# Attention and gated MoE on one core: batches of one row block of four head pairs, and x copied to SBUF

## The chip, the cores and the metric

One NeuronCore of one Trainium2 chip runs the whole program in one launch. The metric is device time in microseconds from the start to the end of one execution. The time before is the median of three runs, 314.85 us, and smaller is better. All data are fp32; the order of the instructions on each engine is fixed when the program is built.

## The reference

Two parts follow one another. The first is causal-local attention with 8 heads over 4 sequences of 768 rows; the second gates a projection of its output by a short causal convolution. Cut to what matters:

```python
# q, k, v: (B=4, H=8, S=768, D=64), n_global = 8, n_local = 96
scores = q @ k.T / 8 ;  rel = row - col
keep = (col < n_global) | ((rel >= 0) & (rel < n_local))
scores += -slope[h] * dist            # dist: |rel|, n_local for global columns
a = softmax(where(keep, scores, -1e9))
x = concat_heads(a @ v)               # (4, 768, 512)
gate = sigmoid(sum_k conv_w[k] * x[t - 4 + k])    # 5 taps, per channel
out = (gate * (x @ w_val)) @ w_out    # (4, 768, 512)
```

## The kernel before

Of each block of 128 rows only a window of 232 columns of the scores is needed: 96 columns before the block, 8 global ones, and the block's own 128. The first block of a sequence needs its own 128 columns alone. One **step** is one row block of one head pair: 4 sequences x 6 blocks x 4 pairs = 96 steps. For each step the two heads' scores go into PSUM, VectorE (DVE) adds the bias and takes the row minimum (`add_bias`, L454; the scores are negated), ScalarE (ACT) takes the exponential with its row sum (`expo`, L464), GpSimd (POOL) or DVE guards the sum (L471), DVE inverts it (L474), POOL or DVE normalises (`norm`, L479), TensorE (PE) transposes (L489 to L495, one PSUM bank), and ACT or DVE copies the transposed p out as `a` (L155 on ACT, L157 on DVE).

A **group** is three steps: three row blocks (half a sequence) of one head pair. Scores (`scores`, L446) and attention times v (`pv`, L515 to L522) run as one batch per group, 32 batches each. From the fifth group on, the `pv` batch of group g - 2 is put directly ahead of the score batch of group g. The result x^T of a group, 128 channels by 384 rows, stands in a single PSUM bank (`x`), with 4 columns of history in front (`hist_in`). From that bank are made:

- `xh`, x rounded to the matmul's float32r (L155 or L157), and `xl`, what rounding left out (L608);
- the five taps of the convolution: the first on ACT or DVE (L618, L620), four on DVE that accumulate into `gate` (L616);
- the last 4 columns, copied to `hist` for the next half.

The bank is free for the next group's `pv` when all of these are done. A **phase** is half a sequence, four groups, 8 phases in all. When a phase's four pairs are there, `val` (L675) is 48 matmuls of 384 columns in three float32r products, ACT applies the sigmoid (L668), DVE multiplies `val` by the gate (L682), the product is split again (`gh`, `gl`, L688), and `out` (L695) is 36 matmuls of 512 columns; the result is copied to `ob` and stored. In the beginning the two weight matrices, given as float64, are converted in eight pieces on DVE, ACT, POOL and PE (L318 to L373).

The order is written by a planner, `Plan.order` (L85): every piece of work has an urgency, a list of what it waits for, and an assumed cost on each engine that may run it; the planner walks in time, gives each engine the most urgent piece that is ready, and chooses the engine that would end it first, with a handicap per engine (`SPARE`). The urgencies of the attention count in steps; those of the MoE part lag by `U_MOE`. The engines then run their lists strictly in that order. `plan.ring` makes a piece wait until a buffer's earlier user is done. All loads and stores go through SyncE's (SP) DMA queue. A run-time flag selects a slow general version for other window sizes, which isn't taken here.

Of the kernel before, what the change touches and what calls it, by code (L numbers as in the profile page):

```python
# [16 lines left out]
WARM = 8  # L17
S_B, PT_B, X_B = 4, 1, 1
U_D1, RAW_B = -6.0, 4
FILL_N, FILL_TO, U_F = 1, 1, -0.27  # L20
W_AT = (2.86, 3, 1.71, 9, 13.7, 16.76, 22, 22.5)
SPARE = {'vector': 0.6, 'gpsimd': -0.44, 'scalar': 0.0}
XH_B, GATE_B, P_B, T_B, A_B, V_B, W_B, WT_B = 7, 2, 5, 8, 9, 4, 2, 1
U_XE, U_XH, U_CV, CV_STEP = 0.7, -1.19, 0.01, 0.32
U_AM, U_EX, U_RC, U_PT, U_EV, U_MOE = 1.02, 1.72, 0.71, 1.89, 2.71, 18
LAG, ALONE = 2, 4
SLACK = 0.01
WO_PE, EARLY, XS_B, U_XO, U_CVE = 0, 0, 6, 0.5, 2.88
# [17 lines left out]
PER = P + NG  # L46
# [4 lines left out]

S_AT = {(k, j): (2 * j + k // 2, k % 2) for k in range(3) for j in range(2)}
# [80 lines left out]
def attention_moe(ctx, tc, qT, kT, kg, vw, v0, v, counts_in, wv, cw, wo, out):  # L133
# [8 lines left out]
    groups = [(b, hf, p) for b in range(B) for hf in range(2) for p in range(NP)]  # L142
    NGRP = len(groups)
    NSTEP = NGRP * HB
# [37 lines left out]
    hist = one.tile([P, NP, HIST], F32, name="hist")  # L182
# [13 lines left out]
    def base(kb):  # L196
        return 0 if kb == 0 else P + PER * (kb - 1)

    def kcols(hf):
        return (0, base(HB)) if hf == 0 else (base(HB) - TAIL, base(NB))  # L200

    def width(s):
        g, k = divmod(s, HB)
        return P if groups[g][1] == 0 and k == 0 else WIN

    def load(g, which):

        b, hf, p = groups[g]
        if which == "rk":
            src, (lo, hi), n = kT[b, p], kcols(hf), 512  # L210
        else:
            src, (lo, hi), n = qT[b, p], (hf * HT, (hf + 1) * HT), HT
        nc.sync.dma_start(tile_of((which, g), [P, n], F32, which, RAW_B)[:, : hi - lo], src[:, lo:hi])

    def load_v0(g):
        b, hf, p = groups[g]
        nc.sync.dma_start(tile_of(("v0", g), [P, 2, D], F32, "v0", 4), v0[b, p])

    def load_v(g):
        b, hf, p = groups[g]  # L220
        t = tile_of(("v", g), [P, HB, 2, 2, D], F32, "v", V_B)
        if hf == 0:
            nc.sync.dma_start(t[:, 1:], vw[b, p, :, : HB - 1])
        else:
            nc.sync.dma_start(t, vw[b, p, :, HB - 1 :])

    for g, (b, hf, p) in enumerate(groups):
        lo, hi = kcols(hf)
        for which, n in (("rk", hi - lo), ("rq", HT)):
            key = ("L" + which, g)  # L230
            plan.add(key, 3 * g + U_L, {SP: 0.5}, lambda e, g=g, which=which: load(g, which),
                     plan.ring(which, RAW_B, key, [("S", g)]), P * n * 4)
        if hf == 0:
            key = ("LV0", g)
            plan.add(key, 3 * g + U_LV, {SP: 0.5}, lambda e, g=g: load_v0(g),
                     plan.ring("v0", 4, key, [("PV", g)]), P * 2 * D * 4)
        key = ("LV", g)
        plan.add(key, 3 * g + U_LV + 0.1, {SP: 0.5}, lambda e, g=g: load_v(g),
                 plan.ring("v", V_B, key, [("PV", g)]), P * (HB - 1 + hf) * 4 * D * 4)
# [12 lines left out]
    for g in range(FILL_TO):  # L252
        for i in range(3):
            plan.add(("F", 3 * g + i), 3 * g + i + U_F, {PE: 0.22 * FILL_N}, lambda e: zeros(FILL_N),
                     [("S", g), ("WARM",)] + [("AM", 3 * g + i, 1)])
# [54 lines left out]
    for h in range(H):  # L310
        for part, cost in enumerate(({DVE: 0.13, POOL: 0.27}, {DVE: 0.19, POOL: 0.36})):
            plan.add(("BIAS", h, part), 3 * (h // 2) + part - 1 + 0.1 * (h % 2), cost,
                     lambda e, h=h, part=part: biases(e, h, part), [("DIST", part)])


    def f64_abs(raw, n, nm):
        y = tile_of((nm, "y"), [P, DM], F32, "wy", WT_B)[:, :n]
        nc.scalar.activation(y, raw[:, :, 1].bitcast(F32), AF.Abs)  # L318

    def f64_op(raw, n, nm, k):  # L320
# [9 lines left out]
        elif k == 2:  # L330
            h = tile_of((nm, "h"), [P, DM], I32, "wh", WT_B)[:, :n]
# [4 lines left out]
        else:  # L336
            r = tile_of((nm, "r"), [P, DM], F32R if by_pe(nm[1]) else F32, "wr", WT_B)[:, :n]
# [37 lines left out]
    def by_pe(i):  # L375
        return i < NC or WO_PE

# [5 lines left out]
    plan.ring("moe", 2, ("WARM",), [("WARM",)] + [("F", s) for s in range(3 * FILL_TO)])  # L383
    for i in range(2 * NC):
# [584 lines left out]
```

## Time and profile before

| | |
|---|---|
| median of three runs | 314.85 us (313.56 to 316.6) |
| the profiled execution | 314.51 us |
| its span on the engines | 312.7 us |
| granted TensorE clock, mean | 0.98 |
| PE busy (matmul) | 287.5 us, 92% |
| DVE busy | 230.8 us, 74% |
| ACT busy | 227.8 us, 73% |
| POOL busy | 148.1 us, 47% |
| DMA | 36.27 MB, mean 116 GB/s |

The profile is of one execution; its times are microseconds from the start of the span. Matmuls overlap in TensorE's pipeline, so their durations add up to more than the time that they take, and the distance between two starts is what one costs. A row of instructions gives start, duration, engine, line, operation, output and input, shape and count; a bracket at its end gives the engine's idle time before it and what ended it. A matmul in fp32 (scores, `pv`, transposes) is counted as two instructions, one in float32r as one.

### The profile page before, as it was taken

To read this page: it belongs to the slowest core of one execution; us is meant where nothing else is said; L and a number is where in the kernel's file an instruction comes from. 1 tells how busy PE (TensorE), PEld (TensorE's weight loads), DVE (VectorE), ACT (ScalarE), POOL (GpSimd) and SP (SyncE) were. 2 spreads that over 40 slices of the span, in tenths; PEclk is the share of its full clock that TensorE was granted. 3 is DMA by queue.
4 is the path that set the end of the run, shared out by engine and by line. 5 is a ranking of instruction groups with operands and counts; after the bars stand their busy time and mean duration, and the time that the engine had idled before them with its cause. 6 is when DMAs were issued, how large, how long until landed. Compare 5 with 4: busy or idle time off the path is not lost.

```text
span 312.7 us, 6857 instructions
## 1 busy us (share of the span) xinstructions
PE 287.5 (92%) x2140; PEld 230.5 (74%) x2140; DVE 230.8 (74%) x819; ACT 227.8 (73%) x634; POOL 148.1 (47%) x333
## 2 busy tenths in 40 slices
PE   8696958798999999999999999999999999999991
PEld 3463746676787777888788778888798778878981
DVE  4778897898678867879685768987698877796210
ACT  3677875996689778987797778877897779865320
POOL 5834556499444734384326442644434542550220
PEclk9999895999999999999999999999999999999998
DMA  6886553313444336313451355323444121001112
GB/s 190 272 275 212 185 170 106 115 51 88 159 128 118 106 101 201 114 47 85 132 189 53 114 155 170 85 85 102 152 146 111 50 85 69 2 2 48 55 39 73
DMA packets 21069, 36.27 MB, mean 116 GB/s; under 512 B 2592, under 2 KB 12832, under 8 KB 21024
## 3 DMA queue, kind: packets, MB, share of 16 engines
q1 hardware_dynamic: 21024, 35.75, 36.9%
q8 instruction: 19, 0.31, 0.4%
q14 instruction: 26, 0.21, 0.2%
HBM read 29.45 MB, written 6.29 MB: 114 GB/s over the span
## 4 chain that ended last, share of the span: by engine, by line
PE 51%; DVE 16%; ACT 14%; POOL 6%; issue 4%; POOLq 0%; ACTq 0%
PE o L695 14%; PE val L675 11%; DVE gate L616 7%; PE s L446 6%; PE x L519 5%; ACT p L464 5%; PE pt L492 4%; PE x L522 4%; POOL p L479 3%; DVE t L454 3%; PE pt L495 3%; DVE xl L608 2%; ACT gate L618 2%; ACT xh L155 1%; ACT gate L668 1%
## 5 line engine op out<-in xcount | busy, mean ns | idle before, releaser
L464 ACT ACTIVATE p<-t,mins 128x232 f32<-128x232 f32 (+1 forms) x192 | 90.4, 472 | 18.2 <-DVE mins L454 16.0
L479 POOL TENSOR_SCALAR p<-p,rs 128x232 f32<-128x232 f32 (+1 forms) x177 | 83.6, 484 | 35.1 <-DVE rs L474 24.7
L616 DVE SCALAR_TENSOR_TENSOR gate<-x,cwt,gate 128x384 f32<-128x384 f32 x128 | 78.2, 611 | 1.9 <-ACT xh L155 1.2
L454 DVE CUSTOM_DVE_ANT_0 t<-s,bias 128x232 f32<-128x232 f32 (+1 forms) x192 | 68.3, 371 | 0.5 <-PE s L446 0.5
L471 POOL TENSOR_SCALAR sm<-sm 128x2 f32<-128x2 f32 x93 | 18.9, 203 | 91.7 <-ACT p L464 87.3
L155 ACT COPY a<-pt 128x464 f32<-128x464 f32 (+1 forms) x87 | 44.6, 513 | 21.1 <-PE pt L495 18.5
L446 PE MATMUL s<-rk,rq 64*128 64x232 f32 (+1 forms) x384 | 47.5, 384 | 1.6 <-DMA rq<-in_qT 1.6
L675 PE MATMUL val<-xh,wvh 128*128 128x384 f32 x128 | 46.8, 366 | 1.4 <-DVE g L682 0.8
L492 PE MATMUL pt<-ident,p 104*128 104x104 f32 x160 | 33.2, 278 | 10.9 <-POOL p L479 9.4
L675 PE MATMUL val<-xh,wvl 128*128 128x384 f32 x128 | 43.2, 337 | 0.0
L675 PE MATMUL val<-xl,wvh 128*128 128x384 f32 x128 | 43.1, 337 | 0.0
L695 PE MATMUL o<-woh,gh 128*128 128x512 f32 x96 | 41.3, 430 | 1.0 <-DVE g L682 1.0
L492 PEld LDWEIGHTS pt<-ident,p 104*128 104x128 f32 x160 | 20.3, 144 | 29.2 <-POOL p L479 17.9
L446 PEld LDWEIGHTS s<-rk,rq 64*128 64x128 f32 x384 | 34.7, 203 | 8.2 <-DVE rs L474 1.9
L695 PE MATMUL o<-wol,gh 128*128 128x512 f32 x96 | 38.0, 396 | 1.4 <-POOL wol L361 1.4
L688 POOL TENSOR_TENSOR gl<-g,gh 128x384 fp32r<-128x384 f32 x30 | 30.5, 1018 | 18.1 <-ACT gh L155 17.2
L695 PE MATMUL o<-woh,gl 128*128 128x512 f32 x96 | 37.8, 394 | 0.0
L474 DVE RECIPROCAL rs<-sm 128x2 f32<-128x2 f32 x96 | 15.8, 164 | 28.2 <-POOL sm L471 27.0
L464 ACT ACTIVATION_READ_ACCUMULATOR p<-t,mins 128x1 f32 x192 | 36.4, 190 | 0.0
L519 PE MATMUL x<-a,v 128*64 128x128 f32 x320 | 33.2, 286 | 0.0
L495 PE MATMUL pt<-ident,p 128*128 128x128 f32 x160 | 31.9, 281 | 0.0
L522 PE MATMUL x<-a,v 104*64 104x104 f32 x320 | 29.0, 260 | 0.0
(164 smaller groups left out, 463.1 us busy)
## 6 DMA issues: line engine op xcount, KB each, us to landing
rq<-in_qT SPq DMA_DIRECT2D x32, 192.0 KB, 3.5
v<-in_vw SPq DMA_DIRECT2D x16, 384.0 KB, 3.2
out<-ob SPq DMA_DIRECT2D x24, 256.0 KB, 2.1
v<-in_vw SPq DMA_DIRECT2D x16, 256.0 KB, 2.8
rk<-in_kT SPq DMA_DIRECT2D x16, 252.0 KB, 3.5
rk<-in_kT SPq DMA_DIRECT2D x16, 200.0 KB, 3.2
w<-in_wv SPq DMA_DIRECT2D x4, 512.0 KB, 4.6
w<-in_wo SPq DMA_DIRECT2D x4, 512.0 KB, 3.7
```

The source lines that it names most:

```text
L155: nc.scalar.copy(dst, src)
L446: nc.tensor.matmul(T["s", g, k, j][:, :n], T["rq", g][r, k * P : (k + 1) * P], T["rk", g][r, c0 : c0 + n], start=True, stop=True)
L454: nc.vector.tensor_tensor_reduce(out=t[:, :n], in0=T["s", s // HB, s % HB, j][:, :n], in1=bias[:, h, :P] if n == P else bias[:, h, P:], op ...
L464: nc.scalar.activation(T["p", s][:, j, :n], T["t", s, j][:, :n], AF.Exp, bias=mins[:, s, j : j + 1], scale=-1.0, accum_out=T["sm", s][:, j ...
L479: engine(e).tensor_scalar(out=pr, in0=pr, scalar1=rs, scalar2=1.0, op0=ALU.mult, op1=ALU.mult)
L492: nc.tensor.transpose(pt[:, j * QA : (j + 1) * QA], pr[:QA, j, :P], ident[:QA, :QA])
L495: nc.tensor.transpose(pt[:, c : c + P], pr[:, j, CA:], ident)
L519: nc.tensor.matmul(head(j, P), T["v", g][:, k, j, 1], a[:, 2 * QA + j * P : 2 * QA + (j + 1) * P], start=True, stop=False)
L522: nc.tensor.matmul(head(j, QA), T["v", g][:CA, k, j, 0], a[:CA, j * QA : (j + 1) * QA], start=False, stop=True)
L616: nc.vector.scalar_tensor_tensor(out=gt, in0=src, scalar=w, in1=gt, op0=ALU.mult, op1=ALU.add)
L675: nc.tensor.matmul(T["val", ph, m], (wvh, wvh, wvl)[r][:, c, m * P : (m + 1) * P], (T["xh", g], T["xl", g], T["xh", g])[r], start=(c == 0 ...
L695: nc.tensor.matmul(T["o", ph, k], (T["gh", ph, c], T["gl", ph, c], T["gh", ph, c])[r][:, cols], (woh, woh, wol)[r][:, c], start=(c == 0 an ...
```

## The change

The groups become **batches** of one row block of all four head pairs: 24 batches of four steps, in the order of the row blocks. Loads of q, k, v come as one transfer per batch each, from arrays that the host lays out so (`qb`, `k0`, `kb`, `vb`, `v0`). A batch of scores fills all eight halves of the four PSUM banks (before: six). `pv` of a batch writes a bank of 128 channels x 4 pairs x 128 rows, and this bank is copied at once to SBUF (`x_out`, 24 copies of 128x512 on ACT or DVE). `xh`, `xl` and the taps are then made from the copy `xs`, which holds a whole phase of three batches with its 4 columns of history; all three may now go to POOL as well, except the four accumulating taps. The convolution of a phase begins when its three batches are copied, and `val` waits for `xh` and `xl` of all three. The matmuls of scores, `pv`, transposes, `val` and `out` keep their shapes and number. The buffers for the weight conversion are taken from `ob`'s ring, and the options `WO_PE` and `EARLY`, which were off, are dropped. All urgencies, handicaps and buffer counts of the planner have other values, with one due time per batch (`U_ATT`) and per phase (`U_CVP`) added.

The core of the diff:

```diff
-U_D1, RAW_B = -6.0, 4
-SPARE = {'vector': 0.6, 'gpsimd': -0.44, 'scalar': 0.0}
-XH_B, GATE_B, P_B, T_B, A_B, V_B, W_B, WT_B = 7, 2, 5, 8, 9, 4, 2, 1
-U_AM, U_EX, U_RC, U_PT, U_EV, U_MOE = 1.02, 1.72, 0.71, 1.89, 2.71, 18
+U_D1, RK_B, RQ_B = -11.96, 3, 3
+SPARE = {'vector': 0.4, 'gpsimd': -1.07, 'scalar': -1.28}
+XH_B, XS_B, GATE_B, P_B, T_B, A_B, V_B, W_B, GL_B, OB_B = 2, 2, 2, 5, 7, 8, 3, 2, 4, 3
+U_AM, U_EX, U_RC, U_PT, U_EV, U_MOE = 1.48, 6.43, -11.79, -13.48, -2.33, 28
...
-    groups = [(b, hf, p) for b in range(B) for hf in range(2) for p in range(NP)]
+    batches = [(b, blk) for b in range(B) for blk in range(NB)]
...
+    def load_k(n):
+        b, blk = batches[n]
+        t = tile_of(("rk", n), [P, NP, WIN], F32, "rk", RK_B)
+        if blk == 0:
+            nc.sync.dma_start(t[:, :, :P], k0[b])
         else:
+            nc.sync.dma_start(t, kb[b, blk - 1])
...
+    def scores(n):
+        banks = [tile_of(("s", n, i), [P, 2, P * 2], F32, "s", S_B, psum) for i in range(4)]
+        w = width(n)
+        for p, j in [(p, j) for p in range(NP) for j in range(2)]:
             r = slice(j * D, (j + 1) * D)
+            x = T["s", n, p, j] = banks[2 * j + p // 2][:, p % 2]
+            nc.tensor.matmul(x[:, :w], T["rq", n][r, p], T["rk", n][r, p, :w], start=True, stop=True)
...
+    def s_deps(n):
+        deps = [("Lrk", n), ("Lrq", n)]
+        return deps + ([("AM", s, j) for s in range(NP * (n - 1), NP * n) for j in range(2)] if n else [])
+
+    def pv_deps(n):
+        deps = [("EV", s) for s in range(NP * n, NP * n + NP)] + [("LV", n)]
+        return deps + plan.ring("x", X_B, ("PV", n), [("XE", n)])
...
-    def x_high(e, g):
-        copy(e, tile_of(("xh", g), [P, HT], F32R, "xh", XH_B), x_of(g)[:, HIST:])
+    def x_out(e, n):
+        ph, _, cols = block(n)
+        copy(e, T["xs", ph][:, :, cols], T["x", n])
+
+    def x_high(e, n):
+        ph, dst, cols = block(n)
+        if n % HB == 0:
+            tile_of(("xh", ph), [P, NP, HT], F32R, "xh", XH_B)
+        copy(e, T["xh", ph][:, :, dst], T["xs", ph][:, :, cols])
...
-        gt, src, w = T["gate", ph][:, p], x_of(g)[:, k : k + HT], cwt[:, p, k : k + 1]
+        gt, src, w = T["gate", ph][:, p], T["xs", ph][:, p, k : k + HT], cwt[:, p, k : k + 1]
...
+            plan.add(key, u + U_XE, {ACT: 0.5, DVE: 0.6}, lambda e, n=n: x_out(e, n), [("PV", n), ("HI", ph)])
+            for name, at, cost, fn in (("XH", U_XH, {ACT: 0.5, DVE: 0.36, POOL: 0.75}, x_high),
+                                       ("XL", U_XL, {DVE: 0.62, POOL: 1.35}, x_low)):
...
+        for p in range(NP):
+            for k in range(TAPS):
+                key = ("CV", ph, p, k)
+                deps = [("CV", ph, p, k - 1)] if k else [("CW",)] + [("XE", n) for n in own]
...
+                plan.add(key, NP * (own[-1] + LAG) + U_CV + U_CVP[ph] + CV_P * p + CV_STEP * k,
+                         {DVE: 0.55} if k else {DVE: 0.37, ACT: 0.4, POOL: 0.75},
...
-                deps = [("XH", ph * NP + c), ("XL", ph * NP + c), ("WP", c), ("WH", c)]
+                deps = [(x, n) for n in range(HB * ph, HB * ph + HB) for x in ("XH", "XL")] + [("WP", c), ("WH", c)]
```

More of the change, by code (lines that the diff above doesn't have):

```diff
@@ L215, in load_v0, with width @@
[L215 to L223, printed above, removed]
-        else:
[L225 to L239, printed above, removed]
+    def width(n):
+        return P if batches[n][1] == 0 else WIN
@@ L554, in attention_moe, with s_cost, pv_cost @@
-    for g, (b, hf, p) in enumerate(groups):
-        for k in range(HB):
-            s = 3 * g + k
-            n = width(s)
-            full = n == WIN
+    def s_cost(n):
+        return (SCORES if width(n) == WIN else 0.22) * NP
+    def pv_cost(n):
+        return (0.395 if width(n) == WIN else 0.22) * NP
+    def s_deps(n):
[4 more added lines that the diff above has]
+        return deps + plan.ring("x", X_B, ("PV", n), [("XE", n)])
@@ new lines, in attention_moe @@
+    for n in range(NBAT + LAG):
+        h = n - LAG
+        u = NP * n + U_S
+        if n < NBAT and n < ALONE:
+            plan.add(("S", n), u, {PE: s_cost(n) + 2 * SWITCH}, lambda e, n=n: scores(n), s_deps(n))
+        if 0 <= h and n < ALONE or n >= NBAT:
+            plan.add(("PV", h), u, {PE: pv_cost(h) + 2 * SWITCH}, lambda e, h=h: pv(h), pv_deps(h))
+        if ALONE <= n < NBAT:
+            plan.add(("PV", h), u, {PE: pv_cost(h) + SWITCH}, lambda e, h=h: pv(h), s_deps(n) + pv_deps(h))
+            plan.add(("S", n), u, {PE: s_cost(n) + 2 * SWITCH}, lambda e, n=n: scores(n), s_deps(n) + [("PV", h)])
+            plan.follow(("S", n), ("PV", h))
@@ L559, in attention_moe @@
+    for n in range(NBAT):
+        for s in range(NP * n, NP * n + NP):
+            p = s % NP
+            full = width(n) == WIN
+            due = s + U_ATT[n]
             for j in range(2):
                 key = ("AM", s, j)
[L561 to L562 removed]
+                plan.add(key, due + U_AM, {DVE: 0.32 if full else 0.21}, lambda e, s=s, j=j: add_bias(s, j),
+                         [("S", n), ("BIAS", 2 * p + j, int(full))] + plan.ring("t", T_B, key, [("EX", s, j)]))
@@ L604, in x_high, with hist_in @@
-    def x_high(e, g):
-        copy(e, tile_of(("xh", g), [P, HT], F32R, "xh", XH_B), x_of(g)[:, HIST:])
-    def x_low(e, g):
-        engine(e).tensor_sub(tile_of(("xl", g), [P, HT], F32R, "xl", XH_B), x_of(g)[:, HIST:], T["xh", g])
-    def conv(e, g, k):
-        ph, p = divmod(g, NP)
+            plan.add(key, due + U_EV, {ACT: 0.5 if full else 0.3, DVE: 0.58 if full else 0.33},
+                     lambda e, s=s: evac_pt(e, s), [("PT", s)] + plan.ring("a", A_B, key, [("PV", n)]))
+    def hist_in(e, ph):
+        x = tile_of(("xs", ph), [P, NP, HIST + HT], F32, "xs", XS_B)
+        if ph % 2 == 0:
+            nc.gpsimd.memset(x[:, :, :HIST], 0.0)
+        else:
+            copy(e, x[:, :, :HIST], T["xs", ph - 1][:, :, HT:])
```

303 lines of the change are left out of this document (117 added, 186 removed).

## The prediction

> **What bounds the kernel now.** I read the page's engine line first, then the span cut into stages, and then the instructions of TensorE one after the other. The columns of the stage rows are: stretch, its length, busy us of PE, weight loads, DVE, ACT and POOL, the granted clock, and the DMA share.
>
> ```profile
> span 312.7 us, 6857 instructions
> PE 287.5 (92%) x2140; PEld 230.5 (74%) x2140; DVE 230.8 (74%) x819; ACT 227.8 (73%) x634; POOL 148.1 (47%) x333
> ...
> 4.90:81.67 76.77, 63.13 (x420) 46.27 (x420) 64.35 (x215) 55.83 (x162) 49.60 (x95) 0.93 0.51 166
> 81.67:145.85 64.18, 62.80 (x516) 51.85 (x514) 50.56 (x191) 52.87 (x150) 31.21 (x77) 1.00 0.41 120
> 145.85:212.26 66.41, 65.53 (x527) 54.15 (x525) 51.01 (x190) 53.03 (x151) 30.01 (x75) 1.00 0.41 120
> ...
> 269.88:306.40 36.52, 36.08 (x224) 30.45 (x222) 18.09 (x50) 16.36 (x37) 9.96 (x16) 1.00 0.11 38
> ```
>
> I cut the stages where the score batch of group 0, 8, 16, 24 and 31 begins, so the first three hold eight groups each (the fourth, with seven, is left out; the last is the tail). From 81.67 us on PE is busy 98 to 99% of the time, eight groups cost 64.2 to 66.4 us, and the tail, nearly all MoE, is full too. **The middle and the tail are bound by PE.** The first stage is not: 76.8 us for eight groups, although it holds fewer PE instructions, 420 against 516 and 527. There DVE has the highest share, 64.35 of 76.77 us (84%), and the clock is 0.93. So a gain can come from two places: PE time itself, or the head.
>
> Next I read a steady group (one score batch and one attention-times-v batch) instruction by instruction. Columns: start, duration, engine, line, tile.
>
> ```profile
> 136.34 0.38 PE L495 MATMUL pt<-ident,p 128*128 128x128 f32 x2
> 136.66 0.44 PE L519 MATMUL x<-a,v 128*64 128x128 f32 x4
> 136.93 0.35 PE L522 MATMUL x<-a,v 104*64 104x104 f32 x4
> 137.11 0.39 PE L519 MATMUL x<-a,v 128*64 128x128 f32 x4
> 137.33 0.35 PE L522 MATMUL x<-a,v 104*64 104x104 f32 x4
> ...
> 137.73 0.35 PE L522 MATMUL x<-a,v 104*64 104x104 f32 x4
> 138.01 1.45 PE L446 MATMUL s<-rk,rq 64*128 64x232 f32 x12
> 139.38 0.40 PE L492 MATMUL pt<-ident,p 104*128 104x104 f32 x2
> 139.62 0.38 PE L495 MATMUL pt<-ident,p 128*128 128x128 f32 x2
> 139.76 0.42 PE L675 MATMUL val<-xh,wvh 128*128 128x384 f32 x1
> ...
> 138.01 0.47 PE L446 MATMUL s<-rk,rq 64*128 64x232 f32 x2
> ```
>
> Starts matter here, because durations overlap. Twelve score instructions last 1.45 us and two last 0.47, so each further pair costs (1.45 - 0.47) / 5 = 0.196 us, and the six pairs need 1.18. Yet the next instruction starts 1.37 us after the batch: 0.19 is lost leaving it. Entering the v batch loses 0.18 (136.66 - 136.34 = 0.32, against 0.14 from the same transpose to `val` at 139.76), its first L519 takes 0.27 to the next start instead of 0.22 (0.05), and the step from L522 to the scores takes 0.28 instead of 0.18 (0.10). Together **0.52 us per group for changing the shape of the array's work**, none of it a wait on another engine.
>
> **The change part by part.**
>
> *Fewer batches.* The 96 steps and their matmuls stay; 32 batches of 3 steps become 24 of 4. Eight times 0.52 us goes from PE: **-4.2 us**. The middle and tail of PE are full, so this is on the path. Bounds: -3.1 if a quarter of it, the eight groups of the head, is covered there by other waits, and -4.2 if all counts. That the number of batches falls is fixed in the code, so it is no rival that this doesn't happen. The new wait: a batch fills all eight halves of the four score banks, so the next scores, and what PE has behind them, wait for eight adds instead of six. A batch will have about 64.18 / 8 x 4 / 3 = 10.7 us for that: 0.
>
> *x in SBUF.* Today the one PSUM bank of x is held through the copies, the low half and five taps of a group, and the next v batch waits for it. After the change it is held for one copy. What comes and goes, by the groups of instructions (busy us, mean ns of one, idle before) and, in the last row, TensorE's wait for that bank:
>
> ```profile
> L616 DVE SCALAR_TENSOR_TENSOR gate<-x,cwt,gate 128x384 f32<-128x384 f32 x128 | 78.2, 611 | 1.9 <-ACT xh L155 1.2 <-ACT hist L155 0.5
> L608 DVE TENSOR_TENSOR xl<-x,xh 128x384 fp32r<-128x384 f32 x32 | 17.7, 554 | 13.4 <-ACT gate L618 13.2
> L155 ACT CAST xh<-x 128x384 fp32r<-128x384 f32 x27 | 12.9, 476 | 13.0 <-PE x L522 12.8
> L155 ACT COPY ob<-o 128x512 f32<-128x512 f32 x15 | 8.6, 576 | 9.4 <-PE o L695 9.4
> L688 DVE TENSOR_TENSOR gl<-g,gh 128x384 fp32r<-128x384 f32 x2 | 1.1, 544 | 0.0
> ...
> PE x L515 <- DVE x L597: 0.9, 1, 0.9
> ```
>
> Added: 24 copies of 128x512 out of PSUM, like the copy of `o` at 576 ns: 13.8 us, on ACT or DVE. The high halves have the same elements in 24 pieces instead of 32; I scale 476 ns by 4/3 as the upper end, 24 x 0.63 = 15.2 against 32 x 0.476 = 15.2, no change; the low halves likewise (0.554 x 4/3 x 24 = 17.7). Removed: 32 small history copies or clears, replaced by 8. The 128 taps after the first read two SBUF tensors; the nearest row is the low half of g on DVE, also 128x384 with two SBUF inputs, 544 ns against 611 now. Consecutive taps already start nearer than 611 apart because they overlap, so I take 0 for the taps and keep -128 x 0.067 = -8.6 us of DVE time as the other end. DVE and ACT at 74 and 73% cover 13.8 us more (4% of the span if all fell on one), so on the path this is 0 in the middle. If that cover were gone, ACT would need 227.8 + 13.8 = 241.6 us, still below PE's 287.5. For the freed bank I take -1, the 0.9 us that a v matmul waited for the clear of x.
>
> *The head.* Here the conv moves. Now it runs group by group amid the attention; after, its 20 operations per phase start when three batches are copied. This is what it displaces now (the DVE rows are one run, of which the score adds and the middle one of three taps are left out; the first row is of TensorE's waits: us, times, longest):
>
> ```profile
> PE pt L492 <- POOL p L479: 9.4, 8, 3.9
> ...
> 42.73 1.55 DVE L338 SCALAR_TENSOR_TENSOR ('w', 4)_r<-w,('w', 4)_y 128x512 f32<-128x512 uint32 x1
> ...
> 44.52 0.61 DVE L616 SCALAR_TENSOR_TENSOR gate<-x,cwt,gate 128x384 f32<-128x384 f32 x1
> ...
> 46.20 0.61 DVE L616 SCALAR_TENSOR_TENSOR gate<-x,cwt,gate 128x384 f32<-128x384 f32 x1
> ...
> 47.49 0.31 PE L492 MATMUL pt<-ident,p 104*128 104x104 f32 x1 [3.94 <-POOL p L479]
> ...
> 36.56 1.57 PE val L675 x9
> ...
> 40.00:50.00 10.00, 5.77 (x44) 4.50 (x44) 9.48 (x29) 6.98 (x20) 6.36 (x10) 0.89 0.46 140
> 50.00:60.00 10.00, 8.13 (x67) 6.52 (x64) 8.16 (x26) 7.45 (x16) 5.69 (x9) 0.77 0.42 139
> ```
>
> Taps and weight conversion stand between the score adds that the whole softmax waits for; PE idles 3.94 us for the normalised p, and in the window after it the clock is 0.77, another 2.3 us. All waits of this kind on p come to 9.4 us. With the first taps only after batch 2, the taps leave this stretch, but the weight conversion stays. I take half of 9.4 and of the 1.1 + 2.3 us of lost clock: -6.4. What stands against it: until batch 2 is copied PE gets no `val` work, where now `val` could start on finished pairs. I price that by the nine `val` matmuls at 36.56 us, 1.57 us in all: +1.6. Together -4.8; I take **-5** for the head; bounds -12 (nearly all of 9.4 + 3.4) and +3 (nothing is won, `val` comes later, the first load is longer).
>
> *Loads.* Fewer, larger transfers, in the same queue. The first scores wait for their load today:
>
> ```profile
> 4.90 2.35 PE L446 MATMUL s<-rk,rq 64*128 64x128 f32 x12 [0.54 <-DMA rq<-in_qT]
> ```
>
> By the shapes in the code the first batch needs 256 + 256 KB instead of 200 + 192, 0.12 MB more; at the head stage's 166 GB/s (last column of the stage rows) that is **+0.7 us**, and at most twice that if the two transfers share the rate with a third. Later loads have the whole batch before as cover, with the DMA engines at 41% in the middle stages.
>
> *POOL beside the taps.* One row pair shows a price that the new taps may have:
>
> ```profile
> 24.46 1.40 POOL L479 TENSOR_SCALAR p<-p,rs 128x232 f32<-128x232 f32 x2 [0.99 <-DVE rs L474]
> 24.94 0.68 DVE L332 SCALAR_TENSOR_TENSOR ('w', 2)_h<-w,('w', 2)_y 128x512 int32<-128x512 int32 x1
> ...
> 264.78 0.89 POOL L479 TENSOR_SCALAR p<-p,rs 128x232 f32<-128x232 f32 x2 [0.69 <-DVE rs L474]
> 264.84 0.61 DVE L616 SCALAR_TENSOR_TENSOR gate<-x,cwt,gate 128x384 f32<-128x384 f32 x1
> ```
>
> A pair of normalisations takes 0.89 us beside a tap that reads x from PSUM, and 1.40 beside an operation with two SBUF inputs: it is held 0.51 us, about as long as that operation lasts. All taps become such operations. In the middle POOL is idle half of the time (31.21 of 64.18 us busy), so I take **+2 us** on PE's path, four full holds; bounds 0 and +12 (the rival below).
>
> The Trainium skill speaks on both sides of this. "GPSIMD Engine Reference", section Specifications, says POOL's SBUF interfaces are shared with VectorE, with contention where a DVE instruction has two SBUF inputs; the 0.89 and 1.40 us agree. "VectorE: DVE Perf Modes", section Rules for kernel authors, advises copying PSUM to SBUF first where many operations follow, and its section on the TRN2 errata has 58 fixed cycles for SBUF sources against 120 for PSUM; by that a tap would be an estimated 65 ns cheaper, 8.3 us of DVE in all, close to the 611 against 544 ns above. By the first rule alone the sum would go towards the second rival below, by the other it would stay, as DVE's time is covered in the middle.
>
> **Sum** against the profiled execution (its own 314.51 us, 1.8 beyond the span; 0.34 below the median shown, so the two bases are the same): -4.2 - 1 - 5 + 0.7 + 2 = -7.5, so **307 us**.
>
> **The rivals.**
>
> *PE was the bound and only the switches go (same).* Head unchanged, POOL's +2: 314.5 - 4.2 + 0.7 + 2 = 313. For it: the longest DVE row ahead of that 3.94 us is weight conversion (1.55 us), which stays. Against: three taps of 0.61 stand there as well. Chance 0.15.
>
> *The taps hold POOL and the transposes come late (slower).* The place is the normalisation ahead of each transpose on PE. Price: up to 0.51 us for each of 96 steps, 49 us at most. The switches less the load gain 3.5, so it is slower by over 1% (+3.5, above 318) when 7 us reach PE, which is 14 steps with the full hold, if the head and the bank win nothing; with their 6 won it takes 26 steps. At 24 held steps and no other gain: 314.5 - 3.5 + 12 = 323; with half of the head's and the bank's, 320. For it: POOL's p is already what PE waits for most. Against: from 81.67 us on PE is 98 to 99% busy, with `val` and `out` to run while a p is late. Chance 0.19.
>
> *The tail opens.* These rows follow the last v batch; PE is full to its last matmul:
>
> ```profile
> 286.76 2.57 DVE L616 SCALAR_TENSOR_TENSOR gate<-x,cwt,gate 128x384 f32<-128x384 f32 x4
> 289.42 1.49 ACT L668 ACTIVATE gate<-gate 128x1536 f32<-128x1536 f32 x1
> ...
> 290.09 7.84 PE val L675 x45
> 297.93 8.42 PE o L695 x36
> ```
>
> Now four taps remain after its copy (2.57 us); after the change sixteen (10.3), then the sigmoid (1.5), then gating, copy and low half (about 0.5 each by the rows of such shapes above), after the copy of x (0.6): 13.9 us. PE has the last `val` in that time (8.4 at 7.84 / 45 for each of 48) and whatever `out` of the phase before is left. If none is left, PE idles 5.5 us: 307 + 5.5 = 312.5. If the whole of it is left (36 at 8.42), nothing is lost; today the tail stage of 36.5 us holds the 16.3 us of these two rows and 20 us of other work, so some is left. Chance 0.06.
>
> **How the numbers follow.** The forecast's own case has 0.60: the switches gone and part or all of the head won, from 314.5 - 4.2 - 12 - 1 = 297 to 311. The first rival and the tail, 0.15 + 0.06, both land at 312 to 313, within 1%, which is about what a measurement of this kernel tells from no change (the three runs shown spread over 1%): same 0.21. The slower rival has 0.19. So faster 0.60, same 0.21, slower 0.19. The range goes from the forecast's lower end, 297, through the two cases within 1%, to the slower rival's 320; what lies beyond is the half of that rival with more held steps and a tenth for a mishap outside all cases. The forecast's own range is 297 to 311.
>
> **What would show it.** Right: 24 score batches; steady stages of twelve steps about 0.5 us shorter than 32.1 to 33.2; no PE wait near 3.9 us on p in the first 70 us, clock near 1.00 there; the x copy at about 0.58 us. Wrong: normalisation pairs above 1.2 us in the middle with PE waiting on p (POOL's rival), an idle PE between the last `val` and the first `out` (the tail), or the first eight batches no earlier than today. What would break the sum most is the order itself: every step's place is worked out by the planner from assumed costs, and a place that I assume covered may not be.

## The result, and the profile after

The changed kernel takes 325.91 us (median of 4 runs, 325.09 to 326.93) against 314.21 for the kernel before on the same chip: a ratio of 1.0361, 95% interval 1.0294 to 1.0428. The forecast was 307, its range 297 to 320; the time lies beyond the range, on the side of the rival that gave 320 to 323.

First the page of after, with the engines' busy time, and the stretches of its span cut where the score batches of steps 0, 24, 48 and 72 begin, the last one ending with the last matmul. The columns are those of the stage rows in the prediction.

```profile
span 324.3 us, 6663 instructions
...
PE 284.2 (88%) x2141; PEld 231.3 (71%) x2141; DVE 222.3 (69%) x729; ACT 233.7 (72%) x636; POOL 217.0 (67%) x387
```

```profile
5.44:67.64 62.20, 48.32 (x361) 35.77 (x361) 48.08 (x176) 47.33 (x145) 50.00 (x94) 0.89 0.61 206
67.64:147.37 79.73, 71.31 (x546) 59.03 (x544) 61.94 (x187) 63.07 (x162) 54.27 (x95) 0.98 0.35 110
147.37:212.20 64.83, 61.94 (x515) 52.52 (x513) 45.89 (x162) 53.58 (x146) 44.16 (x78) 1.00 0.42 135
212.20:317.90 105.70, 98.68 (x719) 82.96 (x718) 65.06 (x201) 67.30 (x181) 66.37 (x110) 1.00 0.22 75
```

Of before, the first three stages stand in the prediction; the fourth, from step 72 to its last matmul, is this:

```profile
212.26:305.94 93.68, 92.10 (x677) 77.15 (x675) 63.87 (x220) 63.68 (x167) 35.16 (x77) 1.00 0.23 74
```

Take PE's busy time from the length of each stage. In the head 13.9 us are left in after and 13.6 in before: the head is 14.6 us shorter, but only because PE has 361 instructions in it instead of 420; no idle time was won. From step 24 on before leaves 1.4 + 0.9 + 1.6 = 3.8 us, after 8.4 + 2.9 + 7.0 = **18.3 us**. That is 14.5 us more, against a loss of 11.7 and 3.3 us that PE is busy less by its row on the page (287.5 to 284.2). POOL, which was busy for 30 to 31 us in each of the second and third stage, now is for 54.3 and 44.2.

What PE's matmuls wait for in that part is in the view of waits (us, times, longest), of after from step 24 on; its five largest rows:

```profile
PE pt L469 <- POOL p L456: 3.8, 6, 0.9
PE pt L469 <- ACT a L155: 3.8, 6, 0.9
PE o L659 <- DVE g L646: 2.3, 2, 1.3
PE val L639 <- DVE g L646: 2.2, 2, 1.4
PE val L639 <- DVE ob L157: 1.8, 2, 1.2
```

The same view of before has four rows, of 1.0 us at most, and none of them names the normalised `p`. Two of them:

```profile
PE o L695 <- DVE g L682: 1.0, 3, 0.5
PE pt L492 <- ACT a L155: 0.9, 2, 0.7
```

No single wait is large in after. What comes through POOL, DVE or ACT is late by about a microsecond at a time. The groups of instructions say why; first after by shape, then the row of before that the prediction does not show (its taps stand there, 611 ns):

```profile
L593 DVE SCALAR_TENSOR_TENSOR gate<-xs,cwt,gate 128x384 f32<-128x384 f32 x128 | 93.6, 741 | 8.5 <-ACT gate L595 5.9 <-POOL gate L597 0.6
L456 POOL TENSOR_SCALAR p<-p,rs 128x232 f32<-128x232 f32 x154 | 91.6, 605 | 20.2 <-DVE rs L451 14.4 <-PE pt L472 0.7 <-PE s L424 0.7
```

```profile
L479 POOL TENSOR_SCALAR p<-p,rs 128x232 f32<-128x232 f32 x145 | 71.1, 503 | 26.7 <-DVE rs L474 19.4 <-PE pt L495 2.6 <-DVE x L597 1.4
```

A tap went from 611 to 741 ns and a normalisation from 503 to 605. The timeline of after shows the meetings (start, duration, engine); the first two rows are one, the next two another, and the last is PE's wait for the `p` of the second:

```profile
156.88 1.27 POOL L586 TENSOR_TENSOR xl<-xs,xh 128x512 fp32r<-128x512 f32 x1 [0.56 <-ACT xh L155]
157.35 1.22 DVE L593 SCALAR_TENSOR_TENSOR gate<-xs,cwt,gate 128x384 f32<-128x384 f32 x1 [2.23 <-ACT gate L595]
...
162.65 1.60 POOL L456 TENSOR_SCALAR p<-p,rs 128x232 f32<-128x232 f32 x2
162.68 1.25 DVE L593 SCALAR_TENSOR_TENSOR gate<-xs,cwt,gate 128x384 f32<-128x384 f32 x2
163.57 0.31 PE L469 MATMUL pt<-ident,p 104*128 104x104 f32 x1 [0.60 <-POOL p L456]
```

One tap lasts 1.22 us beside a low half, and a pair of normalisations 1.60 beside two taps, which themselves are hardly longer (1.25 for both). **Theory A**: taps that read both x and the running sum from SBUF, and POOL's work, hold each other up. **The rivals**: the new order of batches is what costs (B), or POOL's larger load (C).

### The profile page after: what moved, and what is told of

Same layout as the page of the kernel before. It is cut to its first block, busy times and chain, and to the rows that moved or that the text cites. A ratio compares the mean times of both kernels' runs of the same rounds, so it can differ in the third digit from the quotient of the medians.

```text
span 324.3 us, 6663 instructions
## 1 busy us (share of the span) xinstructions
PE 284.2 (88%) x2141; PEld 231.3 (71%) x2141; DVE 222.3 (69%) x729; ACT 233.7 (72%) x636; POOL 217.0 (67%) x387
## 4 chain that ended last, share of the span: by engine, by line
PE 29%; DVE 24%; POOL 19%; ACT 10%; issue 7%; POOLq 0%; ACTq 0%
DVE gate L593 14%; POOL p L456 11%; PE val L639 8%; PE o L659 6%; PE x L493 4%; DVE t L431 4%; PE x L496 3%; POOL sm L448 3%; ACT p L441 3%; PE s L424 3%; PE pt L469 2%; PE pt L472 2%; POOL gl L652 2%; ACT gate L595 1%; POOL xl L586 1%
## 5 line engine op out<-in xcount | busy, mean ns | idle before, releaser
L456 POOL TENSOR_SCALAR p<-p,rs 128x232 f32<-128x232 f32 (+1 forms) x184 | 103.7, 574 | 22.2 <-DVE rs L451 15.1
L593 DVE SCALAR_TENSOR_TENSOR gate<-xs,cwt,gate 128x384 f32<-128x384 f32 x128 | 93.6, 741 | 8.5 <-ACT gate L595 5.9
L431 DVE CUSTOM_DVE_ANT_0 t<-s,bias 128x232 f32<-128x232 f32 (+1 forms) x192 | 61.9, 373 | 5.0 <-ACT p L441 3.8
L155 ACT COPY a<-pt 128x464 f32<-128x464 f32 (+1 forms) x91 | 46.3, 509 | 15.4 <-PE pt L472 13.5
L652 POOL TENSOR_TENSOR gl<-g,gh 128x384 fp32r<-128x384 f32 x32 | 33.7, 1058 | 24.9 <-ACT gh L155 24.3
L469 PE MATMUL pt<-ident,p 104*128 104x104 f32 x160 | 33.2, 276 | 17.5 <-POOL p L456 9.2
L448 POOL TENSOR_SCALAR sm<-sm 128x2 f32<-128x2 f32 x95 | 24.1, 254 | 33.1 <-ACT p L441 26.3
L424 PE MATMUL s<-rk,rq 64*128 64x232 f32 (+1 forms) x384 | 43.2, 366 | 2.4 <-DMA rq<-in_qb 2.4
L469 PEld LDWEIGHTS pt<-ident,p 104*128 104x128 f32 x160 | 19.8, 143 | 35.5 <-POOL p L456 18.5
L493 PE MATMUL x<-a,v 128*64 128x128 f32 x320 | 34.6, 297 | 0.1
L586 POOL TENSOR_TENSOR xl<-xs,xh 128x512 fp32r<-128x512 f32 x22 | 30.6, 1389 | 2.8 <-ACT xh L155 1.9
```

What stands on the lines that cost most here:

```text
L155: nc.scalar.copy(dst, src)
L424: nc.tensor.matmul(x[:, :w], T["rq", n][r, p], T["rk", n][r, p, :w], start=True, stop=True)
L431: nc.vector.tensor_tensor_reduce(out=t[:, :w], in0=T["s", n, p, j][:, :w], in1=bias[:, h, :P] if w == P else bias[:, h, P:], op0=ALU.add, ...
L456: engine(e).tensor_scalar(out=pr, in0=pr, scalar1=rs, scalar2=1.0, op0=ALU.mult, op1=ALU.mult)
L469: nc.tensor.transpose(pt[:, j * QA : (j + 1) * QA], pr[:QA, j, :P], ident[:QA, :QA])
L493: nc.tensor.matmul(head(j, P), v_n[:, p, j, 1], a[:, 2 * QA + j * P : 2 * QA + (j + 1) * P], start=True, stop=False)
```

## The experiments

**x_sbuf_only: the old groups, x in SBUF.** The kernel before has this as an option that was off. It also lets POOL take the high and low halves, the first tap and the small copies.

```diff
-WO_PE, EARLY, XS_B, U_XO, U_CVE = 0, 0, 6, 0.5, 2.88
+WO_PE, EARLY, XS_B, U_XO, U_CVE = 0, 32, 6, 0.5, 2.88
```

> The kernel before with its 32 groups of three blocks kept, and only x copied to SBUF, so that high half, low half and taps read SBUF. Theory A (taps with two SBUF inputs and POOL hold each other up, and that reaches the transposes): slower than before by 5 to 15 us, 320 to 330, taps above 0.70 us, normalisations above 0.57 us. Theory B (the new batches, in which val waits for three batches and a phase's taps come in one run, order the work worse; contention is hidden): within 1% of before, 312 to 318, whatever the taps last.

Measured: 329.68 us, ratio 1.0504 (1.0428 to 1.058). The groups on its page:

```profile
L616 DVE SCALAR_TENSOR_TENSOR gate<-xs,cwt,gate 128x384 f32<-128x384 f32 x128 | 96.7, 756 | 7.5 <-ACT gate L618 5.9
L479 POOL TENSOR_SCALAR p<-p,rs 128x232 f32<-128x232 f32 (+1 forms) x181 | 101.0, 570 | 23.3 <-DVE rs L474 19.4
```

The loss is there without the new batches, and so are both lengthened instructions. B falls as the main cause. C doesn't yet: POOL is busy for 203.7 us here, against 148.1 in before.

**reduce_taps: after, with one SBUF stream per tap.** A sum over the same columns stands in for the tap; the accumulation is left out. Every engine keeps after's order.

```diff
-nc.vector.scalar_tensor_tensor(out=gt, in0=src, scalar=w, in1=gt, op0=ALU.mult, op1=ALU.add)
+nc.vector.tensor_reduce(out=gt[:, k : k + 1], in_=src, op=ALU.add, axis=AX.X)
```

> The changed kernel with the same order; each of the four accumulating taps is replaced by a sum over the same 384 columns of x, which has one SBUF input instead of two (the taps' accumulation is left out). DVE's time for them alone is about the same. Theory A: normalisations return to about 0.50 us, POOL's busy time falls from 217 to 190 us or less, and 8 us or more come back, 310 to 318. Theory B: the time stays at 323 to 327 although the contention is gone.

Measured: 307.29 us, ratio 0.9763 (0.9709 to 0.9817). On its page:

```profile
L593 DVE TENSOR_REDUCE gate<-xs 128x1 f32<-128x384 f32 x128 | 63.3, 541 | 5.1 <-ACT gate L595 4.6
L456 POOL TENSOR_SCALAR p<-p,rs 128x232 f32<-128x232 f32 (+1 forms) x184 | 86.9, 484 | 20.2 <-DVE rs L451 14.0
```

18.6 us come back, more than theory A asked for, and the time lies below its range. The normalisations, which the edit did not touch, fall from 574 to 484 ns (both shapes together), which is what they take in before. The stages, cut as before:

```profile
5.69:64.76 59.07, 45.83 (x360) 34.33 (x361) 44.27 (x175) 46.38 (x145) 47.11 (x95) 0.89 0.62 219
64.76:140.23 75.47, 71.82 (x545) 60.59 (x543) 52.64 (x185) 63.09 (x162) 48.07 (x92) 0.95 0.36 116
140.23:202.00 61.77, 60.99 (x515) 52.79 (x513) 40.12 (x163) 53.61 (x146) 37.91 (x79) 1.00 0.43 142
202.00:299.46 97.46, 96.77 (x720) 83.64 (x718) 54.78 (x201) 66.95 (x181) 56.50 (x110) 1.00 0.23 81
```

From step 24 on PE is now left idle for 3.7 + 0.8 + 0.7 = 5.1 us, against 18.3. But the stand-in is also shorter than a tap, and it writes one column instead of 384, so part of the 18.6 us may be its own. Two controls follow.

**before_reduce and x_sbuf_reduce: the same stand-in in the kernel before and in x_sbuf_only.** The edit is the one above, at L616; in the first the sum reads PSUM, in the second SBUF.

> The kernel before, in which the second to fifth tap of each row becomes the same stand-in as in reduce_taps: a sum over the same 384 columns of x, read from the PSUM bank as before, written to one column of the gate (the accumulation is left out, so the gate is not the reference's). This is the control for reduce_taps: there the stand-in brought 18.6 us, and it may have brought them because it is shorter and writes less, not because it stays out of VectorE's and GpSimd's common way. Theory A (the taps and GpSimd's work hold each other up only where both of the tap's streams are in SBUF): here the taps read one stream from PSUM and were never held, so the stand-in gives at most the 128 x 0.07 us by which it is shorter, mostly off the path: 311 to 315 us, normalisations 480 ns as before. Rival (the stand-in by itself relieves any kernel of some 15 us or more): 295 to 303 us.

> x_sbuf_only (the groups of before, x copied to SBUF for the taps and the halves) with the stand-in of reduce_taps for the second to fifth tap, the sum now read from the copy in SBUF; the accumulation is left out. It fills the fourth field of a table of two by two (x in PSUM or SBUF, true taps or stand-in). Theory A: x_sbuf_only's 14.6 us over before are contention almost alone, so this one returns to 311 to 318 us, normalisations to 480 to 500 ns. Rival (the copies of x, 32 of 0.5 us, and the moved GpSimd work cost the time): it stays at 324 us or more.

Measured: 310.66 us, ratio 0.9875 (0.9849 to 0.9902), and 309.51 us, ratio 0.9851 (0.9812 to 0.989). Both lie just under theory A's ranges, which began at 311, and far from the rivals'. Normalisations on the pages of the two:

```profile
L479 POOL TENSOR_SCALAR p<-p,rs 128x232 f32<-128x232 f32 (+1 forms) x177 | 83.0, 481 | 32.3 <-DVE rs L474 24.5
```

```profile
L479 POOL TENSOR_SCALAR p<-p,rs 128x232 f32<-128x232 f32 (+1 forms) x181 | 87.4, 495 | 20.2 <-DVE rs L474 17.6
```

These two also settle C: x_sbuf_reduce keeps the order of x_sbuf_only, POOL is busy in it for 182.9 us and in reduce_taps for 192.1, against 148.1 in before, and both are faster than before.

The ratios, each to the kernel before measured beside it, in one table:

| | taps as they are | stand-in, one stream |
|---|---|---|
| before (x in PSUM, groups) | 1 | 0.9875 |
| x in SBUF, groups | 1.0504 | 0.9851 |
| after (x in SBUF, batches) | 1.0361 | 0.9763 |

Down the right column no tap has two SBUF streams, and the change gains 0.9875 - 0.9763 = 1.1%, some 3.5 us (0.3 to 1.9% between the ends of the two intervals). Along the rows the stand-in brings 0.0125 where x is in PSUM, 0.0653 and 0.0598 where it is in SBUF: if its own gain is the same in all three rows, the meeting itself costs 0.0653 - 0.0125 = 5.3% (16.6 us) in the groups and 0.0598 - 0.0125 = 4.7% (**14.9 us**) in after. That -3.5 + 14.9 gives the +11.4 us of the ratio 1.0361 is no check of this: the fields of the table make it so. The check is the next pair.

**acc_psum and acc_sbuf: the running sum in a PSUM bank, and back.** What is still wanting is a pair in which the accumulation is done. In acc_psum the taps add up in a bank of their own, which the values and output rows lose (the planner orders anew, with the first tap off POOL); acc_sbuf puts the sum back and keeps all else.

```diff
+        if k == 0:
+            tile_of(("acc", ph, p), [P, DM], F32, "acc", 1, psum)
+        acc = T["acc", ph, p][:, :HT]
+        if k < TAPS - 1:
+            gt = acc
...
-            nc.vector.scalar_tensor_tensor(out=gt, in0=src, scalar=w, in1=gt, op0=ALU.mult, op1=ALU.add)
+            nc.vector.scalar_tensor_tensor(out=gt, in0=src, scalar=w, in1=acc, op0=ALU.mult, op1=ALU.add)
...
-            tile_of(("val", ph, m), [P, HT], F32, "moe", 2, psum)
+            tile_of(("val", ph, m), [P, HT], F32, "moe", 1, psum)
```

> The kernel after with the true computation, but the running sum of a row's taps is kept in a PSUM bank of its own until the last tap writes it to the gate, so that a tap reads one stream from SBUF and one from PSUM. The bank is taken from the two that the values and the output rows share, so these have one; the planner orders anew. Theory A: the taps return to 600 to 640 ns and the normalisations to 480 to 510, although x is read from SBUF as in after. What the lost bank costs is bounded by the rows of after: each of the 56 value and output banks can now make PE wait for its evacuation of some 0.6 us where nothing else is ready, 0 to 34 us, against some 15 us won: 311 to 335 us, with the tap's price as the test and the time as a by-product. Rival (a tap that reads x from SBUF is slow by itself): taps stay at 720 ns or more.

> acc_psum with one thing undone: the running sum of the taps goes back to the gate in SBUF, as in after; the values and output rows keep their one bank, and every engine has acc_psum's order of work. Both do the true computation, so the pair differs in nothing but where the running sum lies. Theory A: taps back at 720 ns or more, normalisations at 560 or more, and the time 8 to 18 us over acc_psum: 368 to 378 us. If the time stays at 358 to 363 us while the taps lengthen, the single bank, not the engines, bounds these two kernels, and the pair prices the instructions alone. Rival (the contention is not in the running sum's place): taps stay at 620 ns.

Measured: acc_psum 360.34 us, ratio 1.146 (1.1411 to 1.151); acc_sbuf 374.8 us, ratio 1.1914 (1.1832 to 1.1996). The groups, first of acc_psum by shape, then on the page of acc_sbuf:

```profile
L456 POOL TENSOR_SCALAR p<-p,rs 128x232 f32<-128x232 f32 x155 | 72.9, 482 | 20.2 <-DVE rs L451 13.5 <-PE val L646 1.2 <-PE pt L472 0.7
L598 DVE SCALAR_TENSOR_TENSOR acc<-xs,cwt,acc 128x384 f32<-128x384 f32 x96 | 59.5, 620 | 16.9 <-ACT acc L600 15.0
```

```profile
L456 POOL TENSOR_SCALAR p<-p,rs 128x232 f32<-128x232 f32 (+1 forms) x187 | 101.7, 556 | 26.8 <-DVE rs L451 18.7
L594 DVE SCALAR_TENSOR_TENSOR gate<-xs,cwt,gate 128x384 f32<-128x384 f32 x128 | 95.3, 749 | 10.0 <-ACT gate L596 7.5
```

With x read from SBUF in both, the place of the running sum alone makes a tap 620 or 749 ns and the kernel 14.5 us slower, about the size in the table. The last tap of a row, which in acc_psum still writes to SBUF, takes 613 ns there: it is the second stream that is read from SBUF, not the writing, that lengthens a tap. Of acc_psum's time the range (311 to 335) was wrong: one bank for the values costs far more than I bounded. It begins step 72 at 196.5 us, where before does at 212.3, but then needs 155 us to its last matmul, against 93.7. Some of this is work put off (852 PE instructions against 677). Some is waiting until the bank is emptied, which two rows of its page show; after has 2.2 us in the place of the first and 2.6 in all in the place of the second:

```profile
L646 PE MATMUL val<-xh,wvh 128*128 128x384 f32 x128 | 48.5, 379 | 16.3 <-DVE g L653 12.3
L666 PE MATMUL o<-woh,gh 128*128 128x512 f32 x96 | 41.8, 436 | 14.4 <-ACT ob L155 11.6
```

No run here isolates what the missing bank costs.

**side_by_side and side_by_side2: the instructions by themselves.** Stages of 24 taps (or another DVE operation) beside 24 normalisations or 12 low halves, on tiles of their own. The main lines:

```diff
+def tap_sbuf(): nc.vector.scalar_tensor_tensor(out=ga, in0=xs[:, 2:386], scalar=w, in1=ga, op0=ALU.mult, op1=ALU.add)
+def norm(): nc.gpsimd.tensor_scalar(out=pr, in0=pr, scalar1=rs, scalar2=1.0, op0=ALU.mult, op1=ALU.mult)
+def low(): nc.gpsimd.tensor_sub(xl, xa, xb)
...
+both(tap_sbuf, norm, 24, 0); both(tap_sbuf, norm, 24, 24); both(tap_psum, norm, 24, 24)
+both(tap_reduce, norm, 24, 24); both(copy_x, norm, 24, 24); both(tap_sbuf, low, 24, 12); both(tap_psum, low, 24, 12)
```

> A program of its own (its output is zeros) that runs, in stages that both engines begin together, 24 taps alone, then 24 taps beside 24 normalisations of 128x232 on POOL: with x from SBUF, with x from PSUM, with a sum over one SBUF input instead, with an SBUF copy of 512 columns; then 24 taps beside 12 low halves of 128x512 on POOL, from SBUF and from PSUM. Theory A: tap alone 0.55 to 0.62 us; beside POOL from SBUF both are stretched, tap and normalisation to a sum near 1.0 to 1.1 us for a pair; from PSUM and for the sum neither is. Theories B and C make no claim on these, only that the stretch is small, below 0.05 us.

> The measurement of side_by_side with its stages held in order. It computes nothing of the reference (the output is zeros); seven stages, each begun by both engines together: 24 taps from SBUF alone; 24 taps from SBUF beside 24 normalisations; 24 taps from PSUM beside 24 normalisations; 24 stand-ins (a sum over SBUF, one stream) beside 24 normalisations; 24 copies of 128x512 from SBUF to SBUF beside 24 normalisations; 24 taps from SBUF beside 12 low halves; 24 taps from PSUM beside 12 low halves. Theory A: alone 0.60 to 0.63 us a tap; from SBUF beside normalisations taps of 0.9 us or more and normalisations of 0.6 or more; from PSUM 0.60 to 0.63 and 0.43 to 0.50; beside the sum no lengthening of either; from SBUF beside low halves taps of 0.9 us or more in the mean. Rival: the SBUF taps are as long alone (0.70 us or more) as beside GpSimd.

In the first the stages ran into one another, so it prices nothing. Of the second, the stretches of the seven stages (columns: DVE busy, POOL busy with counts, then clock, DMA share and GB/s):

```profile
5.60:21.20 15.60, 14.76 (x25) 0.00 (x0) 1.00 1.03 381
21.90:39.40 17.50, 16.66 (x25) 14.99 (x24) 1.00 0.00 1
40.00:55.60 15.60, 14.76 (x26) 10.90 (x24) 1.00 0.00 0
56.10:70.10 14.00, 13.21 (x25) 10.98 (x24) 1.00 0.00 1
70.60:84.80 14.20, 13.39 (x26) 11.97 (x24) 1.00 0.00 0
85.60:111.70 26.10, 25.27 (x25) 17.03 (x12) 1.00 0.00 0
112.20:127.90 15.70, 14.86 (x25) 14.84 (x12) 1.00 0.00 0
```

A tap from SBUF alone takes 14.76 / 24 = 0.615 us, and so does one from PSUM beside normalisations. No stage runs POOL's work alone; its prices are compared with those beside taps from PSUM. Beside normalisations an SBUF tap costs 0.08 more ((16.66 - 14.76) / 24), and the normalisation takes 0.625 instead of 0.454. Beside low halves it is far dearer: 25.27 / 24 = 1.05 us for each tap, or 0.88 us for each low half, which itself takes 1.42 instead of 1.24. Beside the stand-in a normalisation takes 0.457, about as beside taps from PSUM; beside copies of 512 columns, which have one SBUF input, a little more (0.499). So theory A holds, except that a normalisation does not stretch a tap to the 0.9 that it expected.

**low_one_stream: which neighbour costs?** Order kept; the low halves read one stream.

```diff
-engine(e).tensor_sub(T["xl", ph][:, :, dst], T["xs", ph][:, :, cols], T["xh", ph][:, :, dst])
+engine(e).tensor_copy(T["xl", ph][:, :, dst], T["xh", ph][:, :, dst].bitcast(F32))
```

> The kernel after with its order kept; the 24 low halves of x become copies of the high halves (one stream from SBUF instead of two; what is left out is the subtraction, so the low halves are not the reference's). It splits the contention by the neighbour. By side_by_side2 a low half of 1.24 us holds VectorE's taps some 0.87 us (24 taps took 25.27 us beside 12 of them, 14.73 alone), a normalisation some 0.08 us (16.66 beside 24) but is itself lengthened from 0.45 to 0.62 us. Theory A1 (the low halves are what costs): taps at 650 to 670 ns, time 311 to 317 us. Theory A2 (the lengthened normalisations, which PE waits for, cost most): taps at 650 to 670 ns as well, but normalisations still at 580 ns or more and the time at 319 to 325 us. GpSimd also is busy for some 15 us less, which either theory has in it.

Measured: 317.78 us, ratio 1.011 (1.0064 to 1.0157). By shape:

```profile
L456 POOL TENSOR_SCALAR p<-p,rs 128x232 f32<-128x232 f32 x154 | 91.1, 602 | 20.2 <-DVE rs L451 13.3 <-PE s L424 1.1 <-PE x L496 1.0
L593 DVE SCALAR_TENSOR_TENSOR gate<-xs,cwt,gate 128x384 f32<-128x384 f32 x128 | 90.7, 718 | 6.9 <-ACT gate L595 4.2
L586 POOL CAST xl<-xh 128x512 fp32r<-128x512 f32 x22 | 15.9, 721 | 2.6 <-ACT xh L155 2.0
```

8.1 us come back, between the two theories' ranges. The taps stay at 718 ns, which neither expected (650 to 670), and the normalisations at 602. So 8.1 of the 14.9 us hang on the low halves, their 14.7 us of POOL's time (30.6 to 15.9) included; the rest is left, with the normalisations and `gl` (the low half of g, 33.7 us of POOL in after, also with two SBUF inputs) as the taps' neighbours. How much of the 8.1 us is POOL's time and how much the meeting is not told apart, and no run takes `gl` away.

**Four ways around it.** Each lets the planner order anew; of the edits the main lines are shown. x_off_pool keeps `xh`, `xl` and the first tap off POOL; norms_dve keeps the normalisations off it; true_prices gives the planner the durations of after; norm_three does so too and lets ACT normalise.

```diff
 x_off_pool
-("XL", U_XL, {DVE: 0.62, POOL: 1.35}, x_low)
+("XL", U_XL, {DVE: 0.62}, x_low)
 norms_dve
-plan.add(("NM", s, j), due + U_RC + U_NM, {POOL: 0.46 if full else 0.3, DVE: 0.25 if full else 0.15},
+plan.add(("NM", s, j), due + U_RC + U_NM, {DVE: 0.25 if full else 0.15},
 true_prices (a tap: 0.55 to 0.74; the guard on POOL: 0.16 to 0.25)
+plan.add(("NM", s, j), due + U_RC + U_NM, {POOL: 0.6 if full else 0.37, DVE: 0.25 if full else 0.15},
 norm_three
+... {POOL: 0.6 if full else 0.37, DVE: 0.3 if full else 0.2, ACT: 0.42 if full else 0.33},
```

> The changed kernel with high half, low half and first tap taken off POOL's list (ACT and DVE only; the planner orders anew). Theory A: POOL falls to about 170 us, DVE gains some 12 us of work with two SBUF inputs; part comes back, 318 to 324. Theory C (the new load on POOL, an engine in strict order, makes the guard and the normalisation late): nearly all comes back, 311 to 316. Theory B: 322 to 328.

> The kernel after, with the normalisation allowed on VectorE alone (the true computation; the planner orders anew with the same prices). GpSimd loses 184 operations of 574 ns, VectorE takes them on at an estimated 0.25 us each, 46 us. Theory A: with GpSimd's most frequent work gone the taps go from 741 ns to some 650 (the low halves still meet some of them); VectorE is then busy for some 222 + 46 - 12 = 256 us, nearly 80% of the span, and becomes late itself: 312 to 328 us, taps at 620 to 680 ns. Rival (the taps are slow by themselves when they read SBUF): the taps stay at 720 ns or more, and the time rises over 330 us.

> The kernel after with the true computation; only the planner's prices change to what after's trace shows: 0.74 us for a tap (0.55), 0.60 and 0.37 for a normalisation on GpSimd (0.46 and 0.30), 0.25 for the guard of the sum there (0.16). The planner then orders anew and may give VectorE more normalisations. Theory A: the two engines still meet, and the due times were found with the old prices; a better order may hide some of it: 318 to 335 us. Rival (the plan's wrong prices, not the contention itself, cost the time): 312 us or less.

> As true_prices, and a normalisation may also go to ScalarE (a multiplication by the same reciprocal, 0.42 us; the true computation), where no contention with VectorE is to be seen in after. ScalarE has 72% of the span in after. Theory A: what goes to ScalarE no longer meets the taps, taps 690 to 720 ns, but ScalarE's exponentials queue behind it: 312 to 330 us. Rival (GpSimd's load and its queue are what holds the transposes): under 310 us.

Measured: 333.92 us (ratio 1.0613, 1.0547 to 1.0679), 351.76 (1.1192, 1.1173 to 1.121), 330.04 (1.0511, 1.0462 to 1.0561) and 335.31 (1.0677, 1.0609 to 1.0744). All are slower than after. Only true_prices lies in the range expected of it; x_off_pool is above all three of its ranges, norms_dve and norm_three above theory A's. A row of each, in this order, from their pages:

```profile
L456 POOL TENSOR_SCALAR p<-p,rs 128x232 f32<-128x232 f32 (+1 forms) x187 | 109.5, 596 | 26.6 <-DVE rs L451 19.6
```

```profile
PE 287.7 (82%) x2141; PEld 233.2 (67%) x2141; DVE 279.8 (80%) x908; ACT 226.5 (65%) x625; POOL 123.2 (35%) x217
```

```profile
L593 DVE SCALAR_TENSOR_TENSOR gate<-xs,cwt,gate 128x384 f32<-128x384 f32 x128 | 98.1, 773 | 7.9 <-ACT gate L595 5.2
```

```profile
L596 DVE SCALAR_TENSOR_TENSOR gate<-xs,cwt,gate 128x384 f32<-128x384 f32 x128 | 92.4, 734 | 6.9 <-ACT gate L598 4.7
```

In x_off_pool POOL is busy for 187.8 us, less than in reduce_taps (192.1), and the kernel is 26 us slower than that one; the normalisations still take 596 ns and the taps 712. In norms_dve the meetings with normalisations are gone and the taps take 689 ns, so the other neighbours still lengthen them. DVE is now busy for 280 us, and PE's `val` waits 17.6 us for the `g` that DVE makes; the estimate of 256 was too low, as a normalisation there takes 418 ns in the mean and not 250. Better prices in the plan win nothing: the taps are longer still (773 ns). The due times were found with the old prices, so a fresh order may lose something by itself, which these runs don't separate. No version here beats the kernel before with the accumulation done.

## Why the prediction was wrong

**POOL beside the taps is the term that failed.** It had +2 us, "four full holds", with bounds 0 to +12; the runs give +14.9. Three things were wrong in it. It counted only POOL held by DVE, where in side_by_side2 a tap beside low halves also goes from 0.62 to 1.05 us. It looked at the normalisations alone, though the change itself puts 22 low halves with two SBUF inputs on POOL, the worst neighbour measured; the sum had them at DVE's price. And "in the middle POOL is idle half of the time" was read from before: after has POOL busy for 54.27 of 79.73 us there. The row pair that it quoted (0.89 against 1.40) showed the right mechanism; the weight was mine.

**The taps at 0** belong to the same mistake. The nearest row, a low half on DVE at 544 ns with two SBUF inputs, did not show the price: the taps took 741. In side_by_side2 a tap from SBUF alone costs what one from PSUM does (0.615 us), so the 67 ns of gain from that row were not there to have. Nor were the 65 ns that followed from the Trainium skill, "VectorE: DVE Perf Modes", section on the TRN2 errata: no run here shows them. The remark that consecutive taps start nearer than 611 ns apart was misread too: by the tail's own row four of them take 2.57 us, 0.64 each.

**The head at -5** was also wrong, by itself: PE's idle time in the first 24 steps is 13.6 us before, 13.9 after and 13.2 in reduce_taps, and the granted clock fell from 0.93 to 0.89 rather than rising to 1.00. What had looked like a gain is PE work done later.

**The switches at -4.2** fit in size, though no run isolates them: PE's busy time falls by 287.5 - 284.2 = 3.3 us, and without the meeting the whole structure gains 3.5. The price of one is as it was: in after sixteen score instructions begin at 155.44 us and the next matmul at 157.21, which is 0.20 us more than eight pairs at 0.196 need. For the bank (-1) and the first load (+0.7) this leaves about nothing; the scores do start 0.54 us later (5.44 against 4.90). That 307 is also what reduce_taps measures (307.29) is chance: the stand-in gives 3.9 us by itself, which fills the place of the head's 5.

**The rivals.** The second one, "the taps hold POOL and the transposes come late", had the mechanism and a chance of 0.19; its sign that would show it, pairs above 1.2 us with PE waiting on `p` in the middle, is there (1.60 us; the 3.8 us of waits at L469, where before had none). Its price was too low since it saw only normalisations. It also placed the loss at the transposes alone; the waits are spread over `p`, `a`, `g` and `ob`. Its argument against, that PE has `val` and `out` to run meanwhile, did not hold: PE's list is in fixed order. The other two rivals, 312.5 and 313, did not come true; the last stage is longer by 12 us, but reduce_taps with the same order has only 0.7 us of idle time in it, so the tail does not open by its structure, and in after PE is busy for 18.45 of the last 18.50 us, from 299.40 us on, in which the last `val` and `out` lie.

## What to carry to other kernels

Before an operand is moved from PSUM to SBUF, count the operations that then read two tensors from SBUF on VectorE and what GpSimd does meanwhile; the price falls on both engines, and a kernel bound by TensorE still pays it when its waits come through them. A price is to be taken from a row in which the neighbour is running, not from the same instruction alone. When a change has several parts, a stand-in that keeps the order and takes away the suspected property, with its control in the kernel before, sizes that property in two runs; what else the stand-in takes away has to be ruled out by a third.

## What the hardware showed that I had not expected

A VectorE tap with one stream from PSUM and one from SBUF takes 0.615 us beside normalisations and 0.619 beside low halves, no more than a tap with both streams in SBUF takes alone (0.615). Moving only the one stream from PSUM to SBUF makes it 1.05 us beside two-input GpSimd work.

The Trainium skill, "SBUF — State Buffer", section Who interferes with whom, states that a VectorE instruction with two SBUF inputs contends with a GpSimd instruction that reads SBUF, that one with at most one SBUF input outside the two-port modes does not, and that the shared ports are an exclusive lock. On which pairs meet, the runs agree. On the lock they come near it only for low halves: 24 taps and 12 low halves one after the other would be 14.76 + 14.84 = 29.6 us of work, and took 26.1. With normalisations it would be 14.76 + 10.90 = 25.7 us, and took 17.5, so there the two engines overlap for much of the time. Whether the copies, beside which a normalisation took 0.499 us, ran in a two-port mode, no run shows.
